# The stretch behind attention: h loaded into its gradient's place, five turned tiles ahead of w2's turn, stores from SP's queue, and b2's sum on VectorE

## The chip, the cores and the metric

One core of one Trainium2 chip. The metric is device time in microseconds (us) of one execution of the program; a run is one such execution, and the median over the runs counts. Engines: TensorE (PE: matmuls; PEld: its weight loads), VectorE (DVE), ScalarE (ACT), GpSimd (POOL) and SyncE (SP, which here only issues transfers). SP and GpSimd issue transfers (DMAs) from queues of their own; a queue is worked in order, and an instruction that waits holds all behind it.

## The reference, cut to what matters

The program computes an output and the gradients of seven inputs of a block with attention (32 heads of 16) and a gated MLP, for 2048 rows of 512:

```python
xn = _layernorm(x)
s = _A_ref(xn, A_wqkv, A_wo)          # attention, then @ wo
# _B_ref: y = _layernorm(xn); h = gelu(y @ w1 + b1); h @ w2 + b2
g = _silu(_B_ref(xn, B_w1, B_b1, B_w2, B_b2))
out = x + s * g
# then the vjp: gradients of x, wqkv, wo, w1, b1, w2, b2
```

Writing dm for the gradient at h @ w2 + b2, the gradient of b2 is the sum of dm over the 2048 rows, the gradient of w2 is gelu(...)^T @ dm, and the gradient at gelu's input is (dm @ w2^T) times gelu's derivative; the latter is called dh1 here, and its sum over the rows is the gradient of b1.

## The kernel before, in words

The kernel has three stages. The first makes both layer norms, the projections, the MLP forward, and stores to scratch memory what the last stage needs: gelu's input h (H1T_s) and gelu's output (HGT_s), both by pairs of 128 columns and by blocks of 512 rows, 256 KB each; gB (GB_s), two factors per row tile by which the product with wo is multiplied; and others. The second stage is attention, forward and backward, over 16 pairs of heads, and takes most of the time. It ends with stores of dQT (L1652) and dKVT (L1695, four per pair of heads) from GpSimd's queue. Neither stage is touched by the change.

The third stage is `phase3` (from L517), which the change edits. Memory: `k.Oall` and `k.dQall` (128 x 16 x 512 bf16 each) live through attention and `phase3`; attention also uses dQall for some of its maps. `dh1T` (128 x 14 x 2048 bf16) is allocated in `phase3` on memory that attention used. A pool's tile with `bufs=n` has n buffers: the next one waits until the oldest is free. Instructions inside `tc.manual_schedule` (L681 to L827) stand on each engine in the order written; what follows is ordered by a scheduler that may move instructions up between them (in the program before, dQall's turn of L845 and the first dQT load of L839 stand ahead of the last instructions of the hand-ordered part in SP's queue). SP's transfers take turns on eight completion counters, so that each waits for the eighth before it to have landed.

Steps of `phase3` up to the part that isn't touched:

- The *so* loop (L691 to L712), 16 row tiles t. `o_turn` turns a tile of attention's output on TensorE (four 128x128 transposes, copied out by ScalarE); `so` multiplies it with wo (four matmuls), VectorE multiplies the product with gB's halves, giving dm_all[:, t] and t1 (tile t13, two buffers), GpSimd adds x to t1 into ot (ot3, two buffers, one per pair of tiles), and GpSimd's queue stores ot for each pair of tiles (L679). `dm_turn` turns dm_all[:, t-3] into dmT. SP's queue loads gB (gb4, three buffers) and x (x4, three buffers) per pair of tiles, and four pieces of ds4.
- gelu's derivative is made in 28 units (j, g), j a pair of 128 columns, g a block of 512 rows, by `gelu_load` (h from H1T_s; into one of eight slots in dQall, from GpSimd's queue, L569), `gelu_a1`/`a2`, `gelu_b1`/`b2` and `gelu_c` (ScalarE and VectorE), which writes dh1T. Two units are begun in the so loop; later one `gelu_step` stands beside each matmul job.
- hg tiles: `load_hg(j)` (L717) reads gelu's output of pair j turned, in four DMA transposes (L721) from SP's queue, into hgc (three buffers, seven tiles in all).
- b2's gradient: 16 matmuls of a column of ones with dm_all (psdb, L740), copied by ScalarE, stored by GpSimd's queue as one row of 512 (L745).
- dwo (L746 to L754): four jobs of 16 matmuls with ds4. Then `do_dw2(fc)`, 14 jobs of 16 matmuls, jobs 2j and 2j+1 with hg tile j; the first ten run alone, the last four alternate with `dh_tile`. The turned w2 (w2T, L757) is read from SP's queue at job 3, between the hg tiles 3 and 4.
- `dh_tile(gi, fl)` (L782): four times four matmuls of w2T with dmT (ps_dhg), each of which VectorE multiplies into dh1T, with db1's partial sums; then SP's queue turns that part of dh1T into dhc (L791). `dw1_job` multiplies dhc with y. The groups of FC = 14 are FG = 4, 4, 4, 2. At the last group w1 is read turned (w1T, L820).
- b1's sum (L823 to L827), then the product of dh1T with w1T (ps_dy, L853), and the last part (ps_dxa, L905), which needs dQT, wqT, wkvT and R (Rkv, L842), loaded by the list `later`, as is dQall, turned from dQT_s (L845).

Of the kernel before, what the change touches and what calls it, by code (L numbers as in the profile page):

```python
# [510 lines left out]
def phase3(ctx, tc, k, A_x, A_wqkv, A_wo, B_w1, B_w2, grad_out, out_0, out_1, out_2, out_3, out_4, out_5, out_6, out_7, dbg):  # L511
# [14 lines left out]
    with ExitStack() as c1:  # L526
# [13 lines left out]
        base.tile([128, 112], bf16, name="pad_b")  # L540
        dmT = dT.tile([128, IC, S], bf16, name="dmT", tag="dT")

        with ExitStack() as cL:
# [10 lines left out]
            h1s = [k.dQall[:, 2 * n:2 * n + 2, :] for n in range(8)]  # L554
# [81 lines left out]
            def load_gb(h):  # L636

                q4, ts = h // 2, slice(h % 2 * 2, h % 2 * 2 + 2)
                gb4[h] = b2.tile([128, 2, 2, D], bf16, name="gb4", bufs=3)
                if h == 0:  # L640
                    t1s.append(b2.tile([128, D], f32, name="t13"))
                    ots.append(b2.tile([128, 2, D], bf16, name="ot3"))
                nc.sync.dma_start(out=gb4[h][:], in_=k.GB_s[q4, :, ts])
# [22 lines left out]
            def so(t):  # L666
# [6 lines left out]
                t1 = t1s.pop() if t1s else b2.tile([128, D], f32, name="t13")  # L673
# [4 lines left out]
                if t % 2 == 1:  # L678
                    nc.gpsimd.dma_start(out=rows4(o0, t // 4)[:, t % 4 - 1:t % 4 + 1], in_=ot[t // 2][:])  # L679
            ET_ = mybir.EngineType  # L680
            with tc.manual_schedule(engines={ET_.PE, ET_.Activation, ET_.DVE, ET_.SP, ET_.Pool}):  # L681
# [4 lines left out]
                for n in range(3):  # L686
                    gelu_load(n)
# [3 lines left out]
                for t in range(NT):  # L691
# [11 lines left out]
                    if t in (4, 7):  # L703
                        gelu_a1()
                    if t in (5, 8):
                        gelu_a2()
                    if t == 10:
                        gelu_b1(True)
                    if t == 12:
# [22 lines left out]
                def done_dw2(fc, ps):  # L732
                    dw2 = hgp.tile([128, D], bf16, name="dw2", bufs=2)
                    nc.scalar.copy(out=dw2[:], in_=ps[:])
                    nc.gpsimd.dma_start(out=out_6[fc * 128:(fc + 1) * 128, :], in_=dw2[:])
                for j in range(2):
                    load_hg(j)
                psb = psW.tile([1, D], f32, name="psdb2", tag="w")
                for t in range(NT):
                    nc.tensor.matmul(psb[0:1, :], lhsT=ones_bf[:, 0:1], rhs=dm_all[:, t, :], start=(t == 0), stop=(t == NT - 1))  # L740
                db2 = hgp.tile([1, D], bf16, name="db2", bufs=1)
                gelu_c(True)
                gelu_step(True)
                nc.scalar.copy(out=db2[:], in_=psb[:])
                nc.gpsimd.dma_start(out=out_7.rearrange("(o d) -> o d", o=1), in_=db2[:])  # L745
                for ac in range(IC):  # L746
# [5 lines left out]
                    dwo = hgp.tile([128, D], bf16, name="dw2", bufs=2)  # L752
                    nc.scalar.copy(out=dwo[:], in_=ps[:])
                    nc.gpsimd.dma_start(out=out_3[ac * 128:(ac + 1) * 128, :], in_=dwo[:])  # L754
                for fc in range(10):
                    if fc == 3:
                        nc.sync.dma_start_transpose(out=w2T[:], in_=B_w2)  # L757
# [63 lines left out]
                for ic in range(IC):  # L821
                    dw1_job(len(FG) - 1, ic)()
                db1f = b2.tile([128, FC], f32, name="db1f", bufs=1)  # L823
                nc.vector.reduce_sum(out=db1f[:], in_=db1p[:], axis=AX.X)
                db1 = b2.tile([128, FC], bf16, name="db1", bufs=1)
# [15 lines left out]
            def load_r(h):  # L841
                nc.sync.dma_start(out=R[:, 4 * h:4 * h + 4], in_=k.dKVT_s.rearrange("(r p) s -> p r s", p=128)[:, 4 * h:4 * h + 4])  # L842
            later = [lambda: nc.sync.dma_start_transpose(out=wqT[:], in_=A_wqkv[:, 0:D]), lambda: load_dq(0), lambda: load_dq(1),
                     lambda: nc.sync.dma_start_transpose(out=wkvT[:], in_=k.WKVA_s), lambda: load_r(0), lambda: load_r(1),
                     lambda: nc.sync.dma_start_transpose(out=k.dQall[:], in_=k.dQT_s)]  # L845
# [982 lines left out]
```

## Time and profile before

| | us |
|---|---|
| median of 3 runs | 2178.18 |
| lowest, highest | 2175.36, 2189.2 |
| the profiled execution's own time | 2197.41 |
| its span (first to last instruction) | 2195.6 |
| its mean granted TensorE clock | 0.976 |
| busy: PE, DVE, ACT, POOL | 2092.3, 1954.9, 1894.6, 349.9 |

The times in the profile are counted from the span's start; `phase3` begins at about 1850. A row of the chain names, from the end backwards, what each step waited for. In rows of groups, "out<-in" are the program's tile names. A DMA's row is that of its issue; "to landing" is from the issue until its completion is signalled. L numbers are lines of the kernel before; in the changed kernel the same statements stand a few lines lower.

### The profile page before, as it was taken

The page shows a single profiled execution, that of the slowest core. Times are in us where ns is not written, and L with a number is a line of the kernel's source. Part 1 is how long each engine was busy: PE and PEld are TensorE (multiplying, and loading weights), DVE is VectorE, ACT ScalarE, POOL GpSimd, SP SyncE. Part 2 cuts the span into 40 slices and gives each one's busy share as a digit, 9 for nine tenths or more (in the row PEclk, how much of TensorE's full clock was granted, in tenths as well). Part 3 has the DMA queues.
Part 4 walks back from the last instruction along what each step waited for, and adds up shares of the span by engine and source line. Part 5 has one row for each costly group of instructions (what it writes and reads, how often), then busy time and mean ns, then how long its engine had stood idle before and what let it go on. Part 6 is the DMA issues. An engine that isn't in the chain of part 4 may idle for free.

```text
span 2195.6 us, 46078 instructions
## 1 busy us (share of the span) xinstructions
PE 2092.3 (95%) x17683; PEld 749.9 (34%) x17683; DVE 1954.9 (89%) x3485; ACT 1894.6 (86%) x2194; POOL 349.9 (16%) x672
## 2 busy tenths in 40 slices
PE   7999999999999999999999999999999999889999
PEld 3443332333333323323333333233323333334444
DVE  7675999999999999989999999999989997889355
ACT  6667999999999999989999999999989994776233
POOL 4322011111110111111111111120111011520001
PEclk9999999999999999989999999999989998999999
DMA  9884999999999999999999999999999999994971
GB/s 288 273 276 135 226 221 216 228 232 233 226 224 234 222 219 232 230 214 215 234 227 225 229 233 210 229 232 236 227 202 236 221 219 229 264 240 112 181 236 60
DMA packets 1562958, 484.49 MB, mean 221 GB/s; under 512 B 1532432, under 2 KB 1536784, under 8 KB 1562096
## 3 DMA queue, kind: packets, MB, share of 16 engines
q1 hardware_dynamic: 1546256, 441.56, 101.0%
q0 software_dynamic: 12560, 34.74, 6.1%
q10 hardware_dynamic: 3920, 5.24, 0.7%
q8 instruction: 138, 2.26, 0.4%
q14 instruction: 84, 0.69, 0.1%
HBM read 46.52 MB, written 51.12 MB: 44 GB/s over the span
## 4 chain that ended last, share of the span: by engine, by line
PE 64%; DVE 16%; ACT 8%; DMA 7%; issue 3%; SPq 1%; POOL 1%; DVEq 0%; ACTq 0%; POOLq 0%
PE d L1628 13%; PE Z L1663 10%; PE X L1555 9%; DVE gts L1632 8%; PE s L1532 8%; PE t L1542 5%; DMA gk<-gts 4%; ACT e L1550 3%; PE ps_dy L853 2%; PE ps_dhg L787 2%; DVE xs L1587 2%; PE ps_dw L729 2%; DVE eE L1574 2%; ACT et L1546 1%; PE ps_dw L771 1%
## 5 line engine op out<-in xcount | busy, mean ns | idle before, releaser
L1632 DVE TENSOR_TENSOR gts<-d,et 128x512 bf16<-128x512 f32 x1424 | 904.4, 682 | 38.4 <-PE d L1628 19.4
L1546 ACT ACTIVATE et<-s 128x1024 bf16<-128x1024 f32 x712 | 721.6, 1066 | 26.4 <-PE d L1628 15.7
L1628 PE MATMUL d<-dt,KVT 32*128 32x512 bf16 x2048 | 720.7, 388 | 18.3 <-DVE gts L1632 6.4
L1550 ACT ACTIVATE e<-t 128x1024 bf16<-128x1024 f32 x640 | 671.6, 1072 | 29.5 <-PE d L1628 14.8
L1532 PE MATMUL s<-QDT,KVT 32*128 32x512 bf16 x2048 | 403.8, 386 | 23.5 <-ACT e L1550 9.1
L1632 DVE TENSOR_TENSOR gts<-d,dQall 128x512 bf16<-128x512 f32 x624 | 396.7, 682 | 18.3 <-PE d L1628 7.9
L1561 PE MATMUL X<-gts,NAT 128*32 128x512 bf16 x2048 | 407.7, 395 | 0.0
L1671 PE MATMUL Z<-gk,QW 128*32 128x512 bf16 x2048 | 386.1, 396 | 15.8 <-DMA gk<-gts 15.8
L1546 ACT ACTIVATE dQall<-s 128x1024 bf16<-128x1024 f32 x312 | 315.8, 1070 | 11.1 <-PE d L1628 10.1
L1555 PE MATMUL X<-et,NAT 128*32 128x512 bf16 x1424 | 281.4, 392 | 0.8 <-ACT et L1546 0.8
L1542 PE MATMUL t<-KVT,QDT 32*128 32x512 bf16 x1280 | 256.6, 390 | 0.0
L1628 PEld LDWEIGHTS <-KVT 32*128 32x128 bf16 x2048 | 169.1, 91 | 226.8 <-issue 221.7
L1663 PE MATMUL Z<-e,W 128*32 128x512 bf16 x1280 | 243.8, 393 | 0.3 <-DVE xt L1597 0.2
L1532 PEld LDWEIGHTS <-KVT 32*128 32x128 bf16 x2048 | 135.3, 91 | 243.1 <-issue 215.2
L1663 PEld LDWEIGHTS <-W 128*32 128x32 bf16 x2048 | 105.7, 93 | 245.4 <-issue 244.0
L1610 POOL TENSOR_TENSOR On<-xt,rL 128x128 f32<-128x128 f32 x64 | 25.4, 396 | 993.4 <-DVE rL L1601 993.4
L1555 PEld LDWEIGHTS <-NAT 128*32 128x32 bf16 x2048 | 103.0, 95 | 127.1 <-issue 126.9
L1542 PEld LDWEIGHTS <-QDT 32*128 32x128 bf16 x1280 | 82.6, 91 | 140.7 <-issue 128.0
L1555 PE MATMUL X<-dQall,NAT 128*32 128x512 bf16 x624 | 123.6, 392 | 0.0
L1561 PEld LDWEIGHTS <-NAT 128*32 128x32 bf16 x2048 | 100.6, 95 | 63.7 <-issue 57.2
L1663 PE MATMUL Z<-gk,W 128*32 128x512 bf16 x512 | 102.9, 397 | 0.0
L1671 PEld LDWEIGHTS <-QW 128*32 128x32 bf16 x2048 | 89.2, 94 | 25.1 <-DMA gk<-gts 15.5
(223 smaller groups left out, 2621.6 us busy)
## 6 DMA issues: line engine op xcount, KB each, us to landing
gk<-gts SPq DMA_TRANSPOSE x512, 4.5
H1T_s<-h1p SPq DMA_DIRECT2D x28, 256.0 KB, 4.0
dQall<-H1T_s POOLq DMA_DIRECT2D x28, 256.0 KB, 5.0
HGT_s<-hgT SPq DMA_DIRECT2D x21, 256.0 KB, 3.8
NAT_s<-NS SPq DMA_DIRECT2D x4, 1056.0 KB, 5.3
dKVT_s<-ob POOLq DMA_DIRECT2D x64, 64.0 KB, 3.9
gb<-GB_s SPq DMA_DIRECT2D x8, 512.0 KB, 5.9
Rkv<-dKVT_s SPq DMA_DIRECT2D x2, 2048.0 KB, 10.4
```

The lines of the kernel that those rows point to most:

```text
L729: nc.tensor.matmul(ps[:], lhsT=hgc[fc // 2][:, t // 4, fc % 2, t % 4, :], rhs=dm_all[:, t, :], start=(t == 0), stop=(t == NT - 1))
L787: nc.tensor.matmul(ps[:], lhsT=w2T[:, dc, fc * 128:(fc + 1) * 128], rhs=dmT[:, dc, ss], start=(dc == 0), stop=(dc == IC - 1))
L1532: nc.tensor.matmul(s[:, hj, :], lhsT=op["KVT"][r, kb * 128:(kb + 1) * 128], rhs=op["QDT"][r, qc * 512:(qc + 1) * 512], start=True, stop=Tr ...
L1542: nc.tensor.matmul(t[:, hj, :], lhsT=op["QDT"][r, q0:q0 + 128], rhs=op["KVT"][r, kc * 512:(kc + 1) * 512], start=True, stop=True, tile_pos ...
L1546: nc.scalar.activation(out=et_of(g)[:, g % 2], in_=tiles.pop(("s", g))[:], func=ACT.Exp)
L1550: nc.scalar.activation(out=e[:], in_=tiles.pop(("t", u))[:], func=ACT.Exp)
L1555: nc.tensor.matmul(X[32 * hj:32 * hj + 32, :], lhsT=op_of(j)["NAT"][:, kb, hj, 0:32], rhs=et_of(g)[:, g % 2, hj], start=(kb == 0), stop=(k ...
L1561: nc.tensor.matmul(X[64 + 32 * hj:96 + 32 * hj, :], lhsT=op_of(j)["NAT"][:, kb, hj, 1:33], rhs=gts_of(g // 2)[:, g % 2, hj], start=(kb == ...
L1628: nc.tensor.matmul(d[:], lhsT=op_of(j)["KVT"][r, kb * 128:(kb + 1) * 128], rhs=tiles["dt", j][r, :], start=True, stop=True, tile_position= ...
L1632: nc.vector.tensor_tensor(out=gts_of(g // 2)[:, g % 2, hj], in0=tiles.pop(("d", g, hj))[:], in1=et_of(g)[:, g % 2, hj], op=ALU.mult)
L1663: nc.tensor.matmul(cur["Z"][32 * hj:32 * hj + 32, :], lhsT=tiles["W", j][:, qb, hj, :], rhs=rhs_of(tiles["e", j, kc], hj, qb) if e is None ...
L1671: nc.tensor.matmul(cur["Z"][64 + 32 * hj:96 + 32 * hj, :], lhsT=QW[p % 2][:, qc * 4 + qb, hj, :], rhs=rhs_of(tiles["g", j, kc], hj, qb), s ...
```

## The change

The parts of the edit:

- h is loaded straight into dh1T's own place for unit (j, g), where `gelu_c` later overwrites it, and not into slots of dQall. In the so loop the loads go out from SP's queue (three at t = 1, 2, 3, where they stood ahead of the loop before), afterwards from GpSimd's. The first gelu steps in the loop stand two tiles later.
- t13 has four buffers; ot3 keeps two. The store of ot moves from GpSimd's queue to SP's, two tiles behind its pair (`store_o`).
- hg tiles 0, 1, 5 and 6 go into halves of dQall, tiles 2, 3 and 4 into the three hgc buffers. Four tiles are requested ahead of the jobs, tile 4 at job 0, then w2T, then tiles 5 and 6 at jobs 2 and 4.
- b2's gradient is summed by VectorE from dmT, in four parts, during the last four dw1 jobs, and stored from SP's queue element by element (out_7 seen as 128 rows of 4); its matmuls, its copy and its store of one row go.
- dw2 has four buffers. The small tiles of b1's and b2's sums lie in the base pool.
- dQall's turn from dQT_s stands in the hand-ordered part, behind the last dhc turn and behind w1T, ahead of both small stores.

In the built program SP's queue has in this order: wo, three gB and x loads, the first h load, the fourth gB and x load, two h loads, the store of pair 1, and so on. The first h load waits for the stores of dQT and dKVT of the last pair of heads to have landed. The first 20 hg turns stand behind the last store of ot; then w2T, then eight turns. At the end: last dhc turn, w1T, dQall's turn, the stores of b2's and b1's gradients, both dQT loads, wqT, wkvT, two R loads.

```diff
-            h1s = [k.dQall[:, 2 * n:2 * n + 2, :] for n in range(8)]
+            h1_q = [nc.sync]
...
-                    h1 = h1s[made[0] % 8]
                     j, g = gel[made[0]]
-                    nc.gpsimd.dma_start(out=h1, in_=k.H1T_s[j, g])
+                    h1 = dh1T[:, 2 * j:2 * j + 2, g * 512:(g + 1) * 512]
+                    h1_q[0].dma_start(out=h1, in_=k.H1T_s[j, g])
...
-                t1 = t1s.pop() if t1s else b2.tile([128, D], f32, name="t13")
+                t1 = t1s.pop() if t1s else b2.tile([128, D], f32, name="t13", bufs=4)
...
-                if t % 2 == 1:
-                    nc.gpsimd.dma_start(out=rows4(o0, t // 4)[:, t % 4 - 1:t % 4 + 1], in_=ot[t // 2][:])
+
+            def store_o(t):
+                nc.sync.dma_start(out=rows4(o0, t // 4)[:, t % 4 - 1:t % 4 + 1], in_=ot.pop(t // 2)[:])
...
-                for n in range(3):
-                    gelu_load(n)
...
                     so(t)
+                    if t in (1, 2, 3):
+                        gelu_load(t - 1)
...
                     if t >= 3:
                         dm_turn(t - 3)
+                    if t >= 3 and t % 2 == 1:
+                        store_o(t - 2)
...
+                store_o(NT - 1)
                 c2.close()
+                h1_q[0] = nc.gpsimd
...
-                        hgc[j] = hgp.tile([128, 4, 2, 4, 128], bf16, name="hgc")
+                        half = k.dQall[:, 8 * (j % 5):8 * (j % 5) + 8].rearrange("p t d -> p (t d)").rearrange("p (g l t f) -> p g l t f", g=4, l=2, t=4) if j % 5 < 2 else None
+                        hgc[j] = hgp.tile([128, 4, 2, 4, 128], bf16, name="hgc") if half is None else half
...
-                        load_hg(fc // 2 + 2)
+                        load_hg(fc // 2 + 4)
+                    if fc == 0:
+                        nc.sync.dma_start_transpose(out=w2T[:], in_=B_w2)
...
-                for j in range(2):
+                for j in range(4):
                     load_hg(j)
-                psb = psW.tile([1, D], f32, name="psdb2", tag="w")
-                for t in range(NT):
-                    nc.tensor.matmul(psb[0:1, :], lhsT=ones_bf[:, 0:1], rhs=dm_all[:, t, :], start=(t == 0), stop=(t == NT - 1))
...
-                    if fc == 3:
-                        nc.sync.dma_start_transpose(out=w2T[:], in_=B_w2)
...
+                nc.sync.dma_start_transpose(out=k.dQall[:], in_=k.dQT_s)
+                for dc in range(IC):
+                    dw1_job(len(FG) - 1, dc)()
+                    nc.vector.reduce_sum(out=db2f[:, dc:dc + 1], in_=dmT[:, dc, :], axis=AX.X)
+                nc.vector.tensor_copy(out=db2[:], in_=db2f[:])
+                nc.sync.dma_start(out=out_7.rearrange("(c p) -> p c", p=128), in_=db2[:])
...
-                     lambda: nc.sync.dma_start_transpose(out=wkvT[:], in_=k.WKVA_s), lambda: load_r(0), lambda: load_r(1),
-                     lambda: nc.sync.dma_start_transpose(out=k.dQall[:], in_=k.dQT_s)]
+                     lambda: nc.sync.dma_start_transpose(out=wkvT[:], in_=k.WKVA_s), lambda: load_r(0), lambda: load_r(1)]
```

More of the change, by code (lines that the diff above doesn't have):

```diff
@@ L539, in phase3 @@
         db1p = base.tile([128, FC, 4], f32, name="db1p")
-        base.tile([128, 112], bf16, name="pad_b")
+        db1f = base.tile([128, FC], f32, name="db1f")
+        db1 = base.tile([128, FC], bf16, name="db1")
+        db2f = base.tile([128, IC], f32, name="db2f")
+        db2 = base.tile([128, IC], bf16, name="db2")
+        base.tile([128, 32], bf16, name="pad_b")
         dmT = dT.tile([128, IC, S], bf16, name="dmT", tag="dT")
@@ L640, in load_gb @@
                 if h == 0:
-                    t1s.append(b2.tile([128, D], f32, name="t13"))
+                    t1s.append(b2.tile([128, D], f32, name="t13", bufs=4))
                     ots.append(b2.tile([128, 2, D], bf16, name="ot3"))
@@ L702, in phase3 @@
                         gelu_load(6)
-                    if t in (4, 7):
+                    if t in (6, 9):
                         gelu_a1()
-                    if t in (5, 8):
+                    if t in (8, 11):
                         gelu_a2()
-                    if t == 10:
+                    if t == 12:
                         gelu_b1(True)
-                    if t == 12:
+                    if t == 14:
                         gelu_b2()
@@ L751, in phase3 @@
                     gelu_step(True)
-                    dwo = hgp.tile([128, D], bf16, name="dw2", bufs=2)
+                    dwo = hgp.tile([128, D], bf16, name="dw2", bufs=4)
                     nc.scalar.copy(out=dwo[:], in_=ps[:])
```

9 lines of the change are left out of this document (1 added, 8 removed).

## The prediction

> **What bounds the kernel now.** I read the page first, then the chain of waits from 1850 us on, then a table of stretches, then the waits and tiles of the stretch after attention. The page shows one core and a span that the change touches only in its last sixth.
>
> ```profile
> span 2195.6 us, 46078 instructions
> ```
>
> The chain of work that ended last, in order of time (start, length, what), cut to the places that the change touches:
>
> ```profile
> 1860.60 8.43 DMA out_dram<-ot x2
> ...
> 1886.25 5.73 PE psdb L740 x16
> 1891.98 13.92 PE ps_dwo L749 x64
> 1905.90 27.64 PE ps_dw L729 x128
> 1933.54 1.32 SPq L721
> ...
> 1945.56 5.26 DMA hgc<-HGT_s
> ...
> 1950.87 1.04 PE ps_dw L729 x4
> 1951.90 3.45 PE ps_dhg L787 x16
> ...
> 2042.34 0.10 DVE db1p L789
> ...
> 2049.32 10.47 DMA w1T<-in_B_w_dram
> ```
>
> Four places are to be seen. Until 1886.25 the products with wo wait for stores of ot. Then TensorE sums b2's gradient for 5.73 us. From 1933.54 TensorE waits for turned hg tiles: a job of 16 matmuls takes 27.64/8 = 3.45 us, the three jobs up to 1951.90 should take 10.36 and take 18.36, so 8.0 us are lost. Last, w1T's turn lands at 2049.32 + 10.47 = 2059.8, and the products of ps_dy start there. The table of stretches (length; busy us and count of TensorE, its weight loads, VectorE, ScalarE, GpSimd; granted clock; DMA share; GB/s) says who could fill these holes:
>
> ```profile
> 1855.00:1886.25 31.25, 22.78 (x185) 13.39 (x185) 22.26 (x37) 20.79 (x35) 22.75 (x28) 0.96 0.97 335
> 1886.25:1905.73 19.48, 19.48 (x80) 7.89 (x81) 18.59 (x32) 15.94 (x19) 9.43 (x14) 0.89 1.12 243
> 1933.54:1951.90 18.36, 12.72 (x49) 4.76 (x50) 13.89 (x26) 14.68 (x18) 5.23 (x9) 0.91 1.18 246
> 1951.90:2059.84 107.94, 107.30 (x529) 51.33 (x527) 79.45 (x188) 57.07 (x68) 13.46 (x25) 1.00 0.79 180
> ```
>
> No compute engine is full before 1886, while the DMA engines are (0.97), and they are over full (1.12, 1.18) up to 1951.9. So transfers bound the first two holes. From 1951.9 to 2059.84 TensorE itself is full, and all that is gained or lost up to there is only how early the first product with w2T (1951.90, "D" below) can start; the 2195.6 - 1951.9 = 243.7 us behind it move as a block.
>
> **Part 1: the stretch up to 1886 (stores on SP's queue, four t13, h loaded into dh1T).** Waits in 1849 to 1890 (total, times, longest), and the ot tile:
>
> ```profile
> DVE t L674 <- POOL ot L677: 7.3, 5, 3.0
> ```
>
> ```profile
> L677 POOL TENSOR_TENSOR ot<-t,x x16: 1145/1156/1545, 1858.0 to 1888.8; 128x512 bf16<-128x512 f32 x16
> ...
> DMA to landing us min/median/max: 3.7/5.5/7.3
> ```
>
> VectorE waits 7.3 us for GpSimd, and GpSimd waits because ot3 has two buffers: the adds of pair h cannot start before the store of pair h-2 has landed, 5.5 us after its issue (the 8.43 us of the chain are two such landings). Four t13 buffers let VectorE run four tiles ahead, so the 7.3 us go. But ot3 keeps its two buffers, so GpSimd's own cycle stays: two adds, the issue, the landing. And the store now stands in SP's queue, where it has company. In the changed program's order the first h load comes ahead of the fourth gb load, and waits for the last stores of dKVT, since dh1T lies on attention's memory:
>
> ```profile
> 1854.91 1.91 POOL L1695 DMA_DIRECT2D dKVT_s<-ob  x4 [3.17 <-DVE ob L1687]
> ```
>
> ```profile
> dKVT_s<-ob POOLq DMA_DIRECT2D x4, 64.0 KB, 5.2
> ```
>
> Their last is issued at about 1856.3 and lands at 1856.3 + 5.2 = 1861.5. Queued behind that wait are gb, x, two h loads and the first store; each occupies SP for some 0.35 us (below), so this store is issued at about 1863.2, where GpSimd issued it at 1860.60 before. What its landing takes is not shown; SP stores of the same 256 KB earlier in the kernel take 4.0 us, and the ot stores now 5.5; these are my two ends:
>
> ```profile
> H1T_s<-h1p SPq DMA_DIRECT2D x28, 256.0 KB, 4.0
> ```
>
> The store of pair 1 lands at 1867.2 to 1868.7, and pair 3 starts then. A cycle of two adds (2.3), an issue (0.4) and a landing is 6.7 to 8.2 us, so pair 5 starts at 1873.9 to 1876.9 and pair 7 at 1880.6 to 1885.1; pairs 7 and 8 need 4.6 us more, and GpSimd ends at 1885.2 to 1889.7 (1890.0 before). The last store and then the hg turns follow in SP's queue, so turns begin at **1885.6 to 1890.1**. The Trainium skill, DMA: Bandwidth & Descriptors, section "Issuing engines are not separate DMA queues", says that transfers started by any engine run on the same 16 DMA engines and that spreading issuers saves only issue time. By that rule the landing stays near 5.5 us and the late end holds; the stretch's DMA share of 0.97 agrees.
>
> TensorE gets little of VectorE's freedom either. The gb tile's loads (issue ns on SP), and the issues of 1849 to 1960 with their landing:
>
> ```profile
> L643 SPq DMA_DIRECT2D gb<-GB_s x8: 319/320/505, 1850.9 to 1874.2; - x8
> ...
> DMA to landing us min/median/max: 5.2/5.9/8.2
> ```
>
> ```profile
> ds<-DSO_s SPq DMA_DIRECT2D x4, 512.0 KB, 8.2
> ...
> out_dram<-db POOLq DMA_DIRECT2D x1, 1.0 KB, 4.2
> ```
>
> The last gb load stands behind the x load and the store that wait for GpSimd's adds of pairs 4 and 5, goes out at 1873 to 1876 and lands 5.9 later, so the last tiles end at 1881 to 1884.5 (1886.25 before). The fourth ds load stands behind the store of pair 7, goes out at 1883.3 to 1887.8 and lands 5.9 (as gb) to 8.2 us later, 1889.2 to 1896; each of dwo's first 16 matmuls needs its chunk, so the first dwo job ends at 1890 to 1897 (before: 1891.98 + 3.45 = 1895.4). This also takes back what part 2 frees.
>
> **Part 2: b2's sum.** 16 matmuls, 5.73 us, leave TensorE. At 3.45 per job 2.3 us of them are the low clock after a wait (mean 0.89 in the stretch), which dwo would then pay. The rest, 3.4, goes into the wait for ds: worth nothing by itself. On VectorE four sums of 128x2048 come; the nearest row, 0.69 us for 128x512, makes at most 4 x 2.8 = 11 us, in a place where VectorE has nothing:
>
> ```profile
> 2042.90:2059.84 16.94, 16.30 (x107) 10.12 (x106) 0.00 (x0) 3.24 (x7) 3.23 (x6) 1.00 1.15 260
> ```
>
> If that cover were gone, only the stores of db2 and db1 would be late.
>
> **Part 3: five turned tiles ahead of w2T.** SP's queue and its longest wait:
>
> ```profile
> 1880.76 6.92 SPq L721 DMA_TRANSPOSE hgc<-HGT_s  x2
> ...
> 1912.84 5.70 SPq L721 DMA_TRANSPOSE hgc<-HGT_s  x4
> 1918.65 13.24 SPq L757 DMA_TRANSPOSE w2T<-in_B_w_dram  x1
> ```
>
> ```profile
> SPq L721 <- PE ps_dw L729: 5.2, 2, 3.6
> ```
>
> Before, turns start at 1880.76 and D is 1951.90, 71.1 us later; TensorE's job 10 needs tiles 0 to 5 and D follows it, so 24 turns and w2T lie in between. The change does not shorten that list: w2T is moved behind tile 4, yet job 10 still needs tile 5 behind it. What goes is the wait of 3.6 us for tile 0's buffer, since tiles 0 and 1 have dQall and five tiles have room: 67.5. The first two turns took 6.92 us where four later ones took 5.70, because the ds loads were under way; with fewer of these beside them I take up to 4.1 off: 63.4. So D = 1885.6 + 63.4 = 1949.0 to 1890.1 + 67.5 = 1957.6. Best case: 24 turns at 5.70/4 = 1.43, w2T 13.24, the last landing 5.26 and 1.04 of matmuls make 53.8, D = 1939.4, but the DMA share over 1 speaks against it. A second bound is VectorE, whose gelu steps stand ahead of its first product with ps_dhg:
>
> ```profile
> 1886.10 0.42 DVE L621 TENSOR_SCALAR sq<-sq 128x1024 bf16<-128x1024 bf16 x1
> ...
> 1954.03 0.69 DVE L789 CUSTOM_DVE_ANT_0 dh1T<-ps_dhg,dh1T 128x512 bf16<-128x512 f32 x1
> ```
>
> ```profile
> DVE w L585 <- ACT sq L577: 2.9, 2, 1.8
> ```
>
> That is 67.9 us with 2.9 of waiting: 65.0 of work, from 1881 to 1884.5, so 1946 to 1949.5. It hides any faster turning. Between the ends I take D = 1952.4, **+0.5 us**, the turns starting at 1888 and taking 64.4. Four dw2 buffers remove waits of ScalarE, which TensorE did not feel. The h loads and the first gelu steps stand two tiles later in the same order with the same work; seven h loads go out at SP for 0.35 us each and leave GpSimd's queue, which was not what its cycle hung on.
>
> **Part 4: dQall's turn behind w1T, db2 stored element by element.**
>
> ```profile
> 2030.28 10.26 SPq L845 DMA_TRANSPOSE dQall<-dQT_s  x1
> 2041.02 2.02 SPq L791 DMA_TRANSPOSE dhc<-dh1T  x1
> ...
> 2043.72 5.56 SPq L791 DMA_TRANSPOSE dhc<-dh1T  x1
> ...
> 2083.80 1.08 SPq L842 DMA_DIRECT2D Rkv<-dKVT_s  x2
> ```
>
> ```profile
> L905 PE MATMUL ps_dxa<-wkvT,Rkv x128: 378/379/380, 2109.1 to 2187.4; 128*128 128x512 bf16 x128
> ...
> DMA to landing us min/median/max: 8.2/10.4/12.5
> ```
>
> ```profile
> out_dram<-db SPq DMA_DIRECT2D x1, 3.5 KB, 17.6
> ```
>
> dh1T is complete at 2042.4. Without dQall ahead the last dhc turn takes 2.0 instead of 5.56 and ends at 2044.5 instead of 2049.3; w1T follows 4.8 us earlier and TensorE no longer waits for it. In the whole stretch up to 2059.84 TensorE is idle 107.94 - 107.30 = 0.64 us; I take **-0.5 us**. dQall then adds 10.3 us, and db2's store of 512 elements by the 17.6 us of db1's 1792 about 5 (ends 4.2, the store of 1.0 KB before, and 17.6). So R is later by -4.8 + 10.3 + 5 = 10.5 us. Its second load landed at 2084.4 + 12.5 = 2096.9 and is wanted at about 2110: slack 13, still covered: 0. The Trainium skill, DMA: Bandwidth & Descriptors, section "Rules for kernel authors", says that a non-contiguous last dimension becomes one descriptor per element; db1's 3.5 KB in 17.6 us against 1.0 KB in 4.2 agrees.
>
> **Sum.** +0.5 - 0.5 + 0 = 0: the execution of 2195.6 us span stays what it is. Its own time, 2197.41, is 19 us over the median of the runs, 2178.18, and a change of zero carries over: **2178 us**.
>
> **Rivals.** (a) The edits do all they can: stores land in 4.0 us, turning is fast, and VectorE's 1946 sets D. That is -5.9 - 0.5 = -6.4, 2172 us. The waits of 8.0 and 7.3 us speak for it, the unchanged list of turns against it. (b) Slower: SP's queue, now with stores in it, starts the turns at 1890 and nothing speeds them: D = 1957.6, +5.7 - 0.5, 2183 us. It decides when a store's landing is 5.5 us or more. (c) Slower at the end: db2's store takes 17.6 like db1's; R is 23 us later, slack 13, so +10, 2188 us; it decides at over 7.5 us for db2's store. For it speaks that db1's time may be the queue's and not its elements'; against it, the 4.2. (d) No net effect, though each wait moves, is my forecast.
>
> **How the numbers follow.** Forecast within 3 us of 2178: 0.45; (a) and better: 0.22; (b): 0.2; (c): 0.13. The range reaches over (a) to (c) with the spread of the runs shown (2175.36 to 2189.2): 2168 to 2190. About 1%, 21.8 us, is what a measurement here can tell from no change; no case reaches it: faster 0.01, same 0.96, slower 0.03.
>
> **What would show it.** Right: VectorE's wait for ot gone; stores waiting in SP's queue for GpSimd; GpSimd ending near 1888; a wait of TensorE for ds inside dwo; a longer wait for hg tile 5, at job 10 and not at job 8; D within 1949 to 1957; no wait at ps_dxa. Wrong: turns starting before 1884, D before 1946, or TensorE waiting at 2108 for R.

## The result, and the profile after

| | before | after |
|---|---|---|
| median of 20 runs each, us | 2183.76 | 2192.93 |
| lowest, highest | 2171.57, 2198.48 | 2180.66, 2209.96 |
| ratio, 95% interval | | 1.0051 [1.0029, 1.0072] |
| the profiled execution's own time, us | 2197.41 | 2203.78 |

The change makes the kernel slower, by about 11 us by the ratio (6 to 16: 0.0029 and 0.0072 times 2183.76; the medians differ by 9.2). The forecast was no change. Of the 15 us between the forecast, 2178, and 2192.93, 5.6 are not the change's: the kernel before came out at 2183.76 in twenty runs, where three had given 2178.18. The page of after:

```profile
span 2202.0 us, 46024 instructions
```

The spans of the two profiled executions differ by 6.4 us only, because attention, which the change does not touch, happened to end 8.9 us earlier in the later one: the first product with wo stands at 1846.1 instead of 1855.0 (between 1820.8 and 1855.0 in all profiles of this case). So I measure from that product. The kernel falls into four stretches: from there (S) to the first product with w2T (D), to the first product with w1T (Y), to the first product of ps_dxa, to the end. All are read from the first start of a tile's matmuls.

| us | S to D | D to Y | Y to ps_dxa | to the end | sum |
|---|---|---|---|---|---|
| before | 96.7 | 108.1 | 48.4 | 87.4 | 340.6 |
| after | 100.3 | 107.2 | 52.4 | 96.0 | 355.9 |

The loss is in two places: 3.6 us in the first stretch, 12.6 in the last two; 0.9 is gained between. These 15.3 us are those of one profile each, where the runs show about 11.

**The stretch with wo.** SP's queue in after (start, length, line):

```profile
1855.53 0.60 SPq L684 DMA_DIRECT2D out_dram<-ot  x1
...
1859.15 0.32 SPq L647 DMA_DIRECT2D gb<-GB_s  x1
1865.13 0.33 SPq L652 DMA_DIRECT2D x<-in_A_x_dram  x1
...
1870.13 0.57 SPq L647 DMA_DIRECT2D gb<-GB_s  x1
...
1884.74 0.34 SPq L684 DMA_DIRECT2D out_dram<-ot  x1
1885.12 1.35 SPq L731 DMA_TRANSPOSE dQall<-HGT_s  x1
```

The hg turns begin 39.0 us after S (before: 25.7), behind the last store. The queue stands still from 1859.47 to 1865.13: the x load waits for GpSimd's adds, GpSimd for an ot buffer, that buffer for a store. The last gB load, behind all this, goes out 24.0 us after S (19.2 before). The waits in 1840 to 1947:

```profile
DVE dm_all L676 <- DMA gb<-GB_s: 10.0, 3, 4.7
...
POOL ot L681 <- DMA x<-in_A_x_dram: 9.6, 1, 9.6
...
PE ps_dw L741 <- ACT dw L746: 7.1, 1, 7.1
...
PE ps_dwo L755 <- DMA ds<-DSO_s: 2.2, 1, 2.2
```

VectorE's wait for GpSimd (7.3 us before) is gone, and a wait of 10.0 us for gB has come in its place. GpSimd's 9.6 us are put down to an x load, but they end at 1862.8, and that is when the store of 1855.53, which held the ot buffer, landed, 7.2 us after its issue. VectorE's last tile of the loop:

```profile
L678 DVE TENSOR_TENSOR t<-ps_so,gb x16: 676/680/682, 1847.8 to 1879.5; 128x512 f32<-128x512 f32 x16
```

It starts 33.4 us after S, 2.9 later than before (1885.5 - 1855.0 = 30.5). From there the chain of waits of after runs through ScalarE and VectorE by turns:

```profile
1924.02 0.57 ACT dw L746
1924.59 0.96 ACT sq L581
1925.54 0.95 ACT sp L605
1926.50 0.69 DVE dh1T L629
...
1928.17 0.57 ACT dw L746
...
1940.65 0.58 ACT dw L746
...
1941.26 5.32 PE ps_dw L741 x16
1946.59 0.43 PE ps_dhg L791 x2
```

One gelu step takes 1928.17 - 1924.02 = 4.15 us. TensorE's job 10 needs the PSUM buffer that ScalarE's copy of 1940.65 empties, and that copy stands in line behind the gelu steps. No hg turn and no w2T stands in this piece of the chain: in this execution the gelu steps came last.

**The tail.** SP's queue, then the issues of 2045 to 2115 (KB each, us to landing):

```profile
2046.92 9.26 SPq L825 DMA_TRANSPOSE dQall<-dQT_s  x1
2056.28 0.53 SPq L830 DMA_DIRECT2D out_dram<-db  x1
2056.92 0.44 SPq L833 DMA_DIRECT2D out_dram<-db  x1
2057.46 2.96 SPq L845 DMA_DIRECT2D dQT<-dQT_s  x2
2060.78 35.61 SPq L849 DMA_TRANSPOSE wqT<-in_A_wqkv_dram  x1
2096.44 4.30 SPq L850 DMA_TRANSPOSE wkvT<-WKVA_s  x1
2100.84 1.08 SPq L848 DMA_DIRECT2D Rkv<-dKVT_s  x2
```

```profile
dQT<-dQT_s SPq DMA_DIRECT2D x2, 1024.0 KB, 35.9
...
dQall<-dQT_s SPq DMA_TRANSPOSE x1, 18.4
...
out_dram<-db SPq DMA_DIRECT2D x1, 3.5 KB, 32.9
```

b1's store of 3.5 KB takes 32.9 us where it took 17.6, with b2's of 1 KB ahead of it. The dQT loads behind take 35.9, wqT's turn 35.61 only to issue. The R loads leave 47.8 us after Y, instead of 24.6: 23.2 us later. TensorE's wait for them, and a wait of ScalarE, from Y on:

```profile
PE ps_dxa L910 <- DMA Rkv<-dKVT_s: 5.8, 2, 3.9
```

```profile
ACT lnb_z L862 <- remote: 6.7, 1, 6.7
```

and the ten us from ps_dxa's first product on, after and then before (length, five pairs of busy us and count, granted clock, DMA share, GB/s):

```profile
2106.00:2116.00 10.00, 4.18 (x15) 1.33 (x14) 4.25 (x12) 3.58 (x7) 0.00 (x0) 0.80 1.02 419
```

```profile
2108.20:2118.20 10.00, 10.00 (x48) 4.57 (x47) 4.91 (x15) 3.53 (x8) 0.00 (x0) 1.00 0.93 277
```

The wait of 5.8 us costs 96.0 - 87.4 = 8.6, as the granted clock falls to 0.80 there and to 0.86 in the next ten us. The other 4.0 us are in ps_dy, where ScalarE, which empties its PSUM, stood for 6.7 us on something that the trace puts down to no engine of this core; what it was I do not know. The same wait stands at the same statement in e8_tail (1.4 us) and e7_ot3 (1.0), and in no other kernel below. It may have cost nothing of its own: R's second load landed at 2101.4 + 12.4 = 2113.8, and TensorE went on there, so 4.0 us less in ps_dy would have been 4.0 more of waiting for R, unless R's issue hung on ScalarE too.

### The profile page after: what moved, and what is told of

Same layout as the page of the kernel before. It is cut to its first block, busy times and chain, and to the rows that moved or that the text cites. A ratio compares the mean times of both kernels' runs of the same rounds, so it can differ in the third digit from the quotient of the medians.

```text
span 2202.0 us, 46024 instructions
## 1 busy us (share of the span) xinstructions
PE 2087.1 (95%) x17667; PEld 749.7 (34%) x17667; DVE 1966.0 (89%) x3490; ACT 1893.7 (86%) x2193; POOL 345.7 (16%) x656
## 4 chain that ended last, share of the span: by engine, by line
PE 61%; DVE 18%; ACT 9%; DMA 7%; issue 4%; SPq 0%; POOL 0%; another core or an unknown queue 0%; DVEq 0%; ACTq 0%; POOLq 0%
PE d L1633 13%; PE Z L1668 10%; PE X L1560 9%; DVE gts L1637 8%; PE s L1537 8%; PE t L1547 5%; DMA gk<-gts 4%; ACT e L1555 3%; PE ps_dw L775 2%; PE ps_dhg L791 2%; DVE xs L1592 2%; DVE eE L1579 2%; ACT cq L1648 1%; ACT dQall L1551 1%; PE ps_dxa L910 1%
## 5 line engine op out<-in xcount | busy, mean ns | idle before, releaser
L1551 ACT ACTIVATE et<-s 128x1024 bf16<-128x1024 f32 x712 | 719.9, 1062 | 30.4 <-PE d L1633 20.2
L1633 PE MATMUL d<-dt,KVT 32*128 32x512 bf16 x2048 | 715.9, 384 | 18.6 <-DVE gts L1637 6.1
L1555 ACT ACTIVATE e<-t 128x1024 bf16<-128x1024 f32 x640 | 669.0, 1068 | 23.8 <-PE t L1547 13.4
```

The costliest lines, as they stand in the source:

```text
L1551: nc.scalar.activation(out=et_of(g)[:, g % 2], in_=tiles.pop(("s", g))[:], func=ACT.Exp)
L1555: nc.scalar.activation(out=e[:], in_=tiles.pop(("t", u))[:], func=ACT.Exp)
L1633: nc.tensor.matmul(d[:], lhsT=op_of(j)["KVT"][r, kb * 128:(kb + 1) * 128], rhs=tiles["dt", j][r, :], start=True, stop=True, tile_position= ...
```

## The experiments

The theories, as the expectations name them. A: the stores of single elements hold up what stands behind them in the tail. B: dQall's turn, moved behind w1T, does it. C: all is lost in the stretch with wo. S: stores in SP's queue delay the hg turns, and these set D. V: the chain of ScalarE and VectorE sets D. The stretches of all kernels that were timed (us; "turns" and "last tile" count from S to the first hg turn and to the start of VectorE's last t; ratio to the kernel before on the same chip, of 10 to 12 runs each, after of 20 and e2_dq of 6):

| kernel | turns | last tile | S to D | D to Y | Y to ps_dxa | to end | sum | ratio, 95% interval |
|---|---|---|---|---|---|---|---|---|
| before | 25.7 | 30.5 | 96.7 | 108.1 | 48.4 | 87.4 | 340.6 | |
| after | 39.0 | 33.4 | 100.3 | 107.2 | 52.4 | 96.0 | 355.9 | 1.0051 [1.0029, 1.0072] |
| e1_late | 38.5 | 32.8 | 104.0 | 107.2 | 48.3 | 92.2 | 351.7 | 1.0027 [1.0002, 1.0052] |
| e2_dq | 38.7 | 33.1 | 100.7 | 114.7 | 63.5 | 88.5 | 367.4 | 1.0119 [1.0082, 1.0156] |
| e5_pool | 38.8 | 33.2 | 103.7 | 107.1 | 48.4 | 89.5 | 348.7 | 1.0047 [1.0018, 1.0075] |
| e8_tail | 26.3 | 29.2 | 94.4 | 107.1 | 48.4 | 92.3 | 342.2 | 1.0028 [1.0006, 1.0050] |
| e6_gst | 27.8 | 31.3 | 99.5 | 107.1 | 48.4 | 91.5 | 346.5 | 1.0003 [0.9976, 1.0031] |
| e7_ot3 | 32.7 | 30.3 | 96.2 | 107.1 | 48.4 | 89.0 | 340.7 | 0.9987 [0.9967, 1.0007] |
| e9_rows | 38.3 | 32.7 | 99.2 | 107.4 | 48.4 | 87.4 | 342.4 | 1.0006 [0.9982, 1.0031] |
| e10_rows_gst | 28.9 | 32.6 | 99.7 | 107.3 | 48.4 | 87.4 | 342.8 | 1.0000 [0.9976, 1.0024] |
| e11_rows_ot3 | 32.2 | 29.8 | 96.0 | 107.3 | 48.4 | 87.4 | 339.1 | 0.9984 [0.9951, 1.0018] |
| e12_before_rows | 26.1 | 29.5 | 96.4 | 107.3 | 48.4 | 87.8 | 339.9 | 0.9975 [0.9942, 1.0007] |
| e15_db2el | 38.8 | 33.2 | 100.2 | 107.4 | 48.3 | 87.4 | 343.3 | 1.0006 [0.9978, 1.0034] |
| e16_db1el | 38.8 | 33.3 | 101.6 | 107.4 | 48.4 | 87.4 | 344.8 | 1.0007 [0.9975, 1.0038] |

The intervals are about as wide as the whole loss, so the stretches, one profile each, carry the finer readings. How firm these are can be read from kernels that share a stretch. From Y on the sum is 135.7 to 136.2 wherever no transfer behind Y was waited for. From S to D, after, e1_late, e2_dq, e5_pool, e9_rows, e15 to e20 run the same program (e17 to e20 took 100.7, 99.1, 103.2 and 100.3), and they spread from 99.1 to 104.0, median 100.7; e8_tail and e12_before_rows, also alike there, took 94.4 and 96.4. So a difference of 2 us in this stretch is not to be read from one profile; but the two groups, 94.4 to 96.7 with before and 99.1 to 104.0, do not overlap.

### The tail: which transfer is it?

**e1_late**: both small stores behind the R loads.

```diff
-                nc.sync.dma_start(out=out_7..., in_=db2[:])
-                nc.sync.dma_start(out=out_5..., in_=db1[:])
...
+             later = [..., load_r(0), load_r(1), store of db2, store of db1]
```

> The changed kernel with the stores of b2's and b1's sums put behind both R loads in SP's queue; dQall's turn stays where the change put it. Theory A (the element-wise stores, once they stand ahead of dQT, wqT, wkvT and R, hold up everything behind them): the dQT loads land in about 13 us instead of 36, R lands some 20 us earlier, ps_dxa no longer waits for R, ps_dy start to the end of the span falls from 148 to about 136 us, and the time is about 11 us below the changed kernel's, near before (ratio to before 0.999 to 1.002). Rival B (dQall's turn, 10 us, moved behind w1T, is what delays R): dQT and R stay late, the time stays within 3 us of the changed kernel (ratio to before 1.004 to 1.006). Rival C (all of the loss is in the stretch with the products with wo): as B, no gain.

The dQT loads took 7.4 us and R was in time, as A says, but the last stretch still lost 4.8 us:

```profile
xn_all<-XN_s SPq DMA_DIRECT2D x1, 2048.0 KB, 13.2
...
out_dram<-db SPq DMA_DIRECT2D x1, 1.0 KB, 32.6
out_dram<-db SPq DMA_DIRECT2D x1, 3.5 KB, 35.2
```

```profile
PE ps_dwq L883 <- DMA xn_all<-XN_s: 2.9, 1, 2.9
```

The stores take as long as ever and hold up the next load, xn_all (9.1 before). A holds, but moving the stores only moves the harm.

**e2_dq**: dQall's turn ahead of the last dhc turn, as before.

```diff
-                nc.sync.dma_start_transpose(out=k.dQall[:], in_=k.dQT_s)
...
+             later = [..., load_r(1), dQall's turn]
```

> The changed kernel with dQall's turn at the end of the list `later` again, from where the scheduler puts it ahead of the last dhc turn, as in the kernel before; one dQT load then stands ahead of both small stores, the other behind them. Rival B: the time falls by about 11 us to that of before (ratio 0.999 to 1.002), w1T lands about 5 us later against the last dh product. Theory A: the second dQT load still takes over 30 us to land and R lands at least 10 us later than before against the start of ps_dy; ps_dy start to the end stays at 141 to 148 us, ratio to before 1.002 to 1.005.

B is out: the kernel became slower still. The turn goes out earlier, but so do both small stores (22.8 and 30.4 us to landing), beside the last stores of dw1:

```profile
out_dram<-dw POOLq DMA_DIRECT2D x4, 64.0 KB, 28.1
```

```profile
PE ps_dy L858 <- ACT lnb_z L862: 13.2, 1, 13.2
```

The dw1 stores leave from GpSimd's queue and took 28.1 us instead of 12.7 (before) and 6.4 (after). ScalarE waited 25.5 us to reuse their buffer, so it came late to ps_dy's PSUM.

**e5_pool**: both small stores from GpSimd's queue.

```diff
-                nc.sync.dma_start(out=out_7...)      (and out_5)
+                nc.gpsimd.dma_start(out=out_7...)
```

> The changed kernel with both small stores issued from GpSimd's queue at the same place instead of SP's. If the hold-up is the order within SP's own queue (its transfers waiting their turn behind single elements), the dQT loads land in 13 to 18 us again, R is in time, and about 11 us go (ratio to before 0.999 to 1.002). If the single-element writes hold up the 16 DMA engines whichever queue they come from, the dQT loads still take over 25 us, R is still waited for, and the ratio stays at 1.003 to 1.006.

```profile
dQT<-dQT_s SPq DMA_DIRECT2D x2, 1024.0 KB, 32.3
...
out_dram<-db POOLq DMA_DIRECT2D x1, 1.0 KB, 19.1
out_dram<-db POOLq DMA_DIRECT2D x1, 3.5 KB, 31.0
```

The dQT loads leave from SP and are held up as much. So the jam is not in SP's order but in what both queues share; whether that is the DMA engines or the memory behind them, no run here shows.

**e8_tail**: the kernel before with the tail of the change alone (psdb away, b2's sum by VectorE, element-wise store, dQall's turn behind w1T).

> The kernel before with the end of the change alone: b2's sum by VectorE with the element-wise store, no matmuls of b2's sum behind the products with wo, dQall's turn behind w1T; all of the stretch with wo, the hg tiles, the stores and the h loads stay as before. Theory A: nearly the whole loss is here, ratio to before 1.003 to 1.006, dQT loads over 30 us, ps_dxa waiting for R. Rival C (the stretch with wo): ratio 0.998 to 1.001.

The tail loses 4.9 us (92.3 to 87.4) with the stretch with wo untouched; the ratio, 1.0028, is just below what A asks. But 4.9 is not 12.6: with the same tail, after lost 12.6, e8_tail 4.9, e6_gst 4.1, e7_ot3 1.6. The R loads left 47.8, 40.5, 40.5 and 39.4 us after Y; the price hangs on the few us by which R misses.

**e9_rows**: the sums turned by TensorE and stored as 18 rows.

```diff
+                pt = psT.tile([128, IC, 128], bf16, name="db_tp", tag="tp")
+                nc.tensor.transpose(pt[0:IC + FC, 0, :], db12[:], k.ident_bf[:])
+                rows = b2.tile([IC + FC, 128], bf16, name="rows", bufs=1)
+                nc.scalar.copy(out=rows[:], in_=pt[0:IC + FC, 0, :])
+                nc.sync.dma_start(out=out_7.rearrange("(c p) -> c p", p=128), in_=rows[0:IC, :])
+                nc.sync.dma_start(out=out_5.rearrange("(c p) -> c p", p=128), in_=rows[IC:IC + FC, :])
```

> The changed kernel with b2's and b1's sums turned by TensorE (one transpose of 128 by 18) and stored from the same place of SP's queue as 18 rows of 256 bytes instead of 2304 single elements of two bytes. Theory A (single elements): both stores land in under 8 us, the dQT loads in under 16, dQall in under 15, R in time, ps_dxa and the rows behind it do not wait; first product with w1T to the end of the span is 135 to 137 us as before, instead of 148, 140.5 with the stores put last and 138 from GpSimd's queue; ratio to before 1.001 to 1.003, what is left being the stretch with wo. If it is not the elements but the place of the transfers in the queue, the dQT loads stay over 25 us and the ratio at 1.004 to 1.006.

```profile
dQT<-dQT_s SPq DMA_DIRECT2D x2, 1024.0 KB, 6.9
```

The tail is 48.4 + 87.4, as before, with dQall's turn (12.9 us) where the change put it. A is shown, and with it that dQall's move costs nothing. One difference came in with the edit: after has both dQT loads behind the two small stores, but here and in e16_db1el the scheduler put one of them ahead of both, in e15_db2el and e17 to e20 one between them. So the closest comparisons are e16_db1el with e9_rows, and e17 to e20 with e15_db2el.

**e15_db2el, e16_db1el**: e9_rows with one of the two sums stored element by element.

> The changed kernel with b1's sum stored as rows and b2's 512 elements one by one. If the cost goes by the number of elements, this store lands in 6 to 9 us, the dQT loads behind it in 13 to 16, and R is in time: last stretches 136 to 137 us. If a store of single elements of any size holds the loads behind it up, the dQT loads take over 25 us as in the changed kernel.

```profile
dQT<-dQT_s SPq DMA_DIRECT2D x2, 1024.0 KB, 21.1
...
out_dram<-db SPq DMA_DIRECT2D x1, 1.0 KB, 17.3
```

> The mirror image: b2's sum as a row, b1's 1792 elements one by one. By the number of elements: about 18 to 26 us for the store (17.6 before; 33 for 2304 in the changed kernel), the dQT loads 20 to 28, R 8 to 15 us later than with rows, last stretches 136 to 140. If b2's store is the one that does the harm, the last stretches are 136 as with rows and the dQT loads land within 16.

```profile
dQT<-dQT_s SPq DMA_DIRECT2D x2, 1024.0 KB, 14.7
...
out_dram<-db SPq DMA_DIRECT2D x1, 3.5 KB, 18.6
```

512 elements take 17.3 us, 1792 take 18.6: the count hardly matters. R leaves 30.2 and 29.6 us after Y, against 15.2 in e9_rows, so either store alone delays it by some 14 to 15 us. One such store still fits into R's slack (tails 135.7 and 135.8), two do not.

**e17 to e20**: e15_db2el with b2's store changed, one profiled run each.

```diff
e17  out=out_7.rearrange("(p c) -> p c", p=128), in_=db12[:, 0:IC]
e18  out=out_7.rearrange("(c p) -> p c", p=128)[:, 0:2], in_=db12[:, 0:2]
e19  out=out_7.rearrange("(c p) -> p c", p=128)[0:64, :], in_=db12[0:64, 0:IC]
e20  out=out_6[0:IC * 128, 0:1].rearrange("(c p) o -> p (c o)", p=128), in_=db12[:, 0:IC]
```

> As with b1's sum as rows and b2's as elements, but b2's four elements of a partition go to four neighbouring places, so that the store is 128 runs of 8 bytes instead of 512 of two; b2's gradient is then in another order than the reference's. If the number of separate runs sets the 17.3 us, it falls to about 5 to 8 us. If it is the small writes by neighbouring partitions to neighbouring bytes, or a price for any short runs, it stays above 12.

> The same kernel storing only two of the four elements of each of the 128 partitions (256 elements; half of b2's gradient is left out). By elements: 17.3 falls to 9 to 11 us. If the price is by partition, or fixed, it stays at 15 to 18.

> Four elements of each of 64 partitions (256 elements; half of b2's gradient is left out). By partition: half of 17.3, 8 to 10 us, while two elements of each of 128 partitions stay at 15 to 18. By elements: both 9 to 11. Fixed: both 15 to 18.

> The 512 elements of b2's sum go to places 1 KB apart (the first column of the first 512 rows of w2's gradient, which is thereby spoiled, and b2's gradient is left out). If neighbouring two-byte writes collide in memory, the store falls to under 8 us and the dQT loads land within 16; if a single element costs the same wherever it goes, it stays at 15 to 18.

The store's row in each, in this order:

```profile
out_dram<-db SPq DMA_DIRECT2D x1, 1.0 KB, 5.7
```

```profile
out_dram<-db SPq DMA_DIRECT2D x1, 0.5 KB, 15.8
```

```profile
out_dram<-db SPq DMA_DIRECT2D x1, 0.5 KB, 11.0
```

```profile
out_dram<-db SPq DMA_DIRECT2D x1, 1.0 KB, 4.0
```

512 single elements 1 KB apart land in 4.0 us; the same number side by side take 17.3. So a run of two bytes is not dear by itself, nor is it dear that neighbouring partitions write neighbouring runs, if these are of 8 bytes (5.7). Half the elements cost 15.8 with rows of 128 neighbours kept, 11.0 with rows of 64, so neither the number of elements nor that of partitions sets the price alone. What puts all six stores in order is how many pieces fall into one stretch of 256 bytes: 128 of them (18.6, 17.3 and 15.8 us), 64 (11.0), 32 (5.7), one (4.0). This is an ordering of single profiles; a count by 512 bytes gives the same one, and no run varies the stretch by itself. The Trainium skill, DMA: Bandwidth & Descriptors, section Specifications, says that below 512 bytes the engines read, modify and write; colliding writes would fit that, but the 4.0 us show that short writes alone are not slow, and no run here shows the reading.

### The stretch with wo: what sets D?

**e6_gst**: the stores of ot on GpSimd's queue again. **e7_ot3**: `bufs=3` for ot3, nothing else.

```diff
e6   -    nc.sync.dma_start(...)  in store_o, two tiles behind
e6   +    nc.gpsimd.dma_start(...), right behind the pair's adds
e7   -    name="ot3")
e7   +    name="ot3", bufs=3)
```

> The changed kernel with the stores of ot issued from GpSimd's queue again, right behind each pair's adds, as before; the tail stays as changed. Theory S (the stores standing in SP's in-order queue, with two ot3 buffers and landings of 7 us, delay the first hg turn, and the turns with w2T set the first product with w2T): the turns start 26 to 29 us after the first product with wo instead of 38.5 to 39; the first product with w2T comes 94 to 98 us after it instead of 100 to 104; ratio to before about 1.002 to 1.004, the tail's loss still in it. Rival V (VectorE and ScalarE's gelu chain sets that time, so an earlier turn changes nothing): still 100 us or more, ratio 1.004 to 1.006. The theory that all is lost in the tail also expects no change here.

> The changed kernel with three ot3 buffers instead of two, nothing else. If the two buffers are what holds GpSimd (9 to 15 us of waits for the stores), these waits fall to under 4 us, the last store goes out about 33 us after the first product with wo instead of 38, the turns start there, the first product with w2T comes at 97 to 100 us; ratio to before 1.002 to 1.004. If the order of SP's queue and the DMA load of the stretch are what holds it, the turns still start at 37 us or later and the ratio stays at 1.004 to 1.006.

In e6_gst the turns start 27.8 us after S, as S asks, but D falls to 99.5 only, within the spread of the changed kernel. In e7_ot3 they start later than that, at 32.7, and D falls to 96.2, below what was expected:

```profile
L678 DVE TENSOR_TENSOR t<-ps_so,gb x16: 676/680/683, 1845.4 to 1873.7; 128x512 f32<-128x512 f32 x16
```

Its last tile is earlier: 1873.7 - 1843.4 = 30.3, against 31.3 in e6_gst and 33.4 in after.

**e10_rows_gst**: e6_gst and e9_rows together. **e11_rows_ot3**: e7_ot3 and e9_rows. **e12_before_rows**: e8_tail with rows.

> Both mends: the stores of ot from GpSimd's queue, and b1's and b2's sums stored as rows. Theory A with S: both losses go; the first product with w2T at 94 to 98 us after the first product with wo, 107 to the first product with w1T, 135 to 137 to the end; ratio to before 0.996 to 1.000. If either theory is wrong, the ratio stays above 1.001.

> The changed kernel with both sums stored as rows and three ot3 buffers. From the stages measured one by one (96.2 us from the first product with wo to the first with w2T with three buffers, 107.1 from there to the first with w1T, 135.8 from there to the end with the rows) the sum is 339.1 us, 1.5 below the kernel before (340.6): ratio 0.997 to 1.001. Were the two losses one and the same thing (each mend taking the same microseconds), the sum would stay at 341 to 343.

> The kernel before with b2's sum by VectorE and both sums stored as rows, dQall's turn behind w1T; the stretch with wo, the stores, the h loads and the hg turns as before. Stage by stage: 94.4 (as measured where only the tail was changed), 107.1, 135.8: 337.3 us, 3.3 below before, ratio 0.997 to 1.000. This is the part of the change that should gain; were removing b2's matmuls worth nothing, as the prediction had it, the first stage would be 96.5 to 97 and the sum 339.5 to 340.

e9_rows and e10_rows_gst differ in this stretch only by the queue of the stores; the first hg turns:

```profile
L730 SPq DMA_TRANSPOSE dQall<-HGT_s x8: 1308/1768/6842, 1870.8 to 1890.6; - x8
```

```profile
L729 SPq DMA_TRANSPOSE dQall<-HGT_s x8: 1309/2128/3889, 1857.8 to 1875.6; - x8
```

They begin 38.3 and 28.9 us after S, and D is 99.2 and 99.7. So 9.4 us of earlier turns are worth nothing by themselves, and S alone falls. The chain of e10_rows_gst ends with ScalarE's copy, as that of after does:

```profile
1921.85 0.58 ACT dw L744
...
1922.47 6.25 PE ps_dw L739 x16
```

V holds as a bound that no earlier turn gets below: in ten of the fourteen kernels D lies 65.2 to 67.6 us behind VectorE's last tile, and in none does it come sooner. But V is not the only bound. Of the eleven kernels that share the changed stretch, the chain ends with ScalarE's copy in four (after, e9_rows, e15_db2el, e18_half_cols) and with a turned tile in the other seven, among them the three latest, e1_late, e5_pool and e19_half_rows (71.2, 70.5 and 70.0 behind the last tile). This is the tile of e1_late:

```profile
1943.34 8.42 DMA dQall<-HGT_s
```

In before, too, a turned tile came last, though D lies 66.2 behind the last tile there. So in the changed stretch the two bounds end close together, and of what was tried only the third ot3 buffer, which brings both forward (last tile 30.3 and 29.8, turns 32.7 and 32.2), gains: 96.2 and 96.0, where the eleven lie at 99.1 or more.

The mends add up: e11_rows_ot3 has the sum expected, 339.1. It, e7_ot3 and e12_before_rows lie below 1, but their intervals hold 1, so none is shown to beat the kernel before; all three beat the changed kernel, with whose interval theirs do not overlap. With b2's matmuls away and the rest of the stretch as before, D is 0.3 us (e12_before_rows) and 2.3 us (e8_tail) earlier than in the one profile of before: what the matmuls cost lies within the spread of this stretch.

## Why the prediction was wrong, point by point

**Forecast: no net change, 2178.** It was slower by 11 us. Two steps failed, and the larger is the mechanism of rival (c), to which I gave 0.13.

**Part 4, b2's store: the step that failed most.** I priced 512 elements at 5 us, between 4.2 (1 KB as one row) and 17.6 (b1's 1792 elements), by their number. Alone it takes 17.3 (e15_db2el). Rival (c) said exactly that: as dear as b1's, R 23 us later, slack 13, 10 us lost. R left 23.2 us later, and the runs split this as rival (c) did: with b1's elements alone (e16_db1el) R leaves 29.6 us after Y, 5.0 later than before, near the -4.8 + 10.3 of my sum, and b2's elements add 18.2. Of the 12.6 us that the profile of after lost, 5.8 are the wait for R, and 4.0 stood in ps_dy, where they may have hidden as much of that wait; the other 2.8, with the low clock behind the wait, stood in no case of mine, so that 10 came near is partly luck. I had both prices in rows and leaned to the wrong neighbour: the row of 4.2 was a store of the same size, but b1's was one of the same form. What also failed is the size of R's delay in my sum, 10.5; the two stores also hold up dQall's turn (18.4 instead of 13.4) and wqT.

**Part 4, the rest, was right.** I took 0.5 us for w1T, and D to Y fell by 0.9, from 108.1 to 107.2. dQall's turn behind w1T: free (e9_rows).

**Part 1: the second step that failed.** I had the last tiles end at 1881 to 1884.5, 26 to 29.5 us after S, earlier than before (31.2). They ended at 1879.5 + 0.7 = 1880.2, 34.1 after S. The cycle was as I described it (two ot3 buffers, VectorE's wait gone, a wait for ds in dwo, stores waiting in SP's queue), but its first store landed 7.2 us after its issue, where I took 4.0 to 5.5, and I carried its stalls to the hg turns and not far enough to the gB loads in the same queue: the last went out 24.0 us after S instead of my 18 to 21, and landed slower:

```profile
DMA to landing us min/median/max: 4.6/7.0/7.7
```

7.0 where I took 5.9. This is the tile gb in after. A third ot3 buffer, which lets GpSimd run on, takes the 3 us back (e7_ot3, e11_rows_ot3); the stores on GpSimd's queue again do not (last tile 32.6 in e10_rows_gst, 32.7 in e9_rows). The turns began 39.0 us after S, later than my latest, 35.1.

**Part 3: two bounds, and I let one go.** I let the list of 24 turns and w2T set D and named VectorE's gelu work as a second bound, 65.0 us from the end of the last tile to VectorE's first product with ps_dhg. In the profile of after the second came last, and took 1947.5 - 1880.2 = 67.3. Had I used my 65.0 with the last tile where it really ended, D would have come out about 2 us late (34.1 + 65.0 = 99.1 after S, against 96.7), of the 3.6 measured. That D, 100.3 after S, still lies between my ends (94.0 to 102.6) is luck: the turns began 3.9 us later than my latest, and from there to D it took 61.3 us instead of 63.4 to 67.5. Where they start late and also run slowly, they come last, which is rival (b); its 0.2 describes e1_late and e5_pool (104.0 and 103.7), which run the same stretch as after.

**Part 2 was right within the spread**: without psdb D is 0.3 and 2.3 us earlier (e12_before_rows, e8_tail); VectorE's four sums took 2.28 us each where nothing waited.

**Rival (a)**: no kernel here reached it. The best first stretch with hg turned early is 96.0, 0.7 below before.

Not tried: the order of the hg turns and w2T by itself, and gB loaded on another queue than x. Open: ScalarE's 6.7 us in ps_dy, what jams behind the short writes, and over how many bytes they have to be spread.

## What to carry to other kernels

Price a transfer by the nearest row of the same form, not of the same size, and ask first how many short pieces of different partitions fall into the same few hundred bytes; a small result that lies across the partitions can be turned on TensorE and stored as rows. Where two bounds for one event lie within a few us, write both as functions of the same earlier event and recompute both when that event moves. A load that waits for a buffer holds every load behind it in its queue: here an x load, waiting for GpSimd's adds, held gB's, and taking the stores out of that queue did not help (last tile 32.6 instead of 32.7), while one more buffer for GpSimd did (29.8).

## What the hardware showed that I had not expected

- A store of 512 two-byte elements takes 4.0 us when they lie 1 KB apart and 17.3 when they lie side by side from 128 partitions; as 128 runs of 8 bytes, 5.7.
- While such stores are under way, other transfers crawl, also those of the other queue: with both stores ahead, loads of 1 MB took 28.5 to 35.9 us instead of 6.9, and in e2_dq stores of 64 KB 28.1 instead of 5.1 to 12.7. In after the core's DMA engines moved 2 to 35 GB/s (means of 4 us) from 2060 to 2088, and 264 from 2052 to 2056.
- The same store's harm varies: the tail lost 1.6 to 12.6 us with the same instructions. A wait of TensorE of 1.8 us cost 2.1 (e5_pool, clock 1.00 behind it), one of 2.6 cost 4.9:

```profile
2079.70:2089.70 10.00, 7.38 (x27) 2.87 (x26) 4.27 (x13) 3.70 (x9) 0.00 (x0) 0.83 1.02 406
```

This is e8_tail, from ps_dxa's first product on, with the granted clock at 0.83. The Trainium skill, TensorE: Matmul & The Clock Gate, section "Part 1: The HAM clock gate (the "warmup" mystery)", puts the fall of the clock behind an idle window of about 3.4 us; here 2.6 us of waiting sufficed.
